# Scoring the first three heads one step earlier in an attention and soft mixture-of-experts kernel

## The chip, the cores and the metric

The kernel runs on one core of a Trainium2 chip. The metric is the time of one execution on the device in microseconds (us); less is better. The engines are named TensorE (PE in the rows; its weight loads PEld), VectorE (DVE), ScalarE (ACT) and GpSimd (POOL); SyncE (SP) issues most of the transfers.

## What is computed

Three stages follow each other, all in float32. The change lies in the first, causal attention with a decay, for 4 batches of 8 heads (32 heads, 576 positions, width 64):

```python
scores = scale * np.matmul(q, k.transpose(0, 1, 3, 2))
cum = np.cumsum(np.log(np.clip(f, 0.0001, 1.0)), axis=-1)
decay = cum[:, :, :, None] - cum[:, :, None, :]
scores = np.where(causal, -1000000000.0, scores + decay)
scores = scores - np.max(scores, axis=-1, keepdims=True)
attn = np.exp(scores)
attn = attn / (np.sum(attn, axis=-1, keepdims=True) + 1e-09)
out = np.matmul(attn, v)
```

The 2304 rows of the result (512 wide) go through a dense layer with a gate (`h * sigmoid(h)`, 2048 wide inside) and then through a soft mixture of 8 experts with 4 slots each. These two stages are not touched.

## The kernel before

**Heads come in pairs.** A pair p holds heads 2p and 2p + 1. Each pair has tiles that hold the operands of the score products over 128 partitions: `QA` and `KA` (partitions 0 to 63 the rounded queries and keys; above them rows for the decay and constant rows; partition 127 of `QA` is the **row of maxima**, which subtracts each row's maximum inside the product), and `QB` and `KB`, which hold what the rounding left over. There are three buffers of each, taken in turn (`p % 3`).

- `split_hi(p, j)` (L189) fills the rounded parts on ScalarE: j = 0 is `QA`, 1 is `KA`, 2 is `KB`; j = 3 copies `QA`'s queries into `QB` with a DMA of 288 KB. For pair 0, j = 0 makes four copies of half the size and the two copies of the decay rows (`decays_out`).
- `split_lo(p, which, h)` (L205) makes one head's remainder on GpSimd, for `QB` (which = 0) or `KB` (which = 1).
- `init_q(i)` (L133) fills buffer i of `QA`: the pad with zeros on VectorE, and partitions 64 to 127 with a DMA from buffer i - 1. That copy takes the row of maxima of buffer i - 1 along, although it is always written again before it is used.
- `spread(p)` (L213) fetches the decay rows of `KA`; from pair 2 on it reads them from `cumd`, a copy of the sums in device memory (L1127).
- `load(p)` (L169) and `load_v(p)` (L179) fetch queries and keys (576 KB) and values (320 KB).

**The work on a head.** `max_piece(i, j)` (L224), six pieces, multiplies block by block, and VectorE takes each row's maximum from the product's bank. `max_fin` (L247) transposes the maxima of a finished head (from pair 2 on of a pair) on TensorE, has VectorE copy them out as the tile `mr` and sends them by DMA (L255, 512 B a row) into partition 127 of `QA`. `s_piece(i, j)` (L265), five pieces, makes the scores, two products each, and ScalarE takes their exponential (L285). It reads all of `QA`'s partitions and so needs the row of maxima. `cut` (L295) puts zeros above the diagonal on GpSimd. `row_sums(p)` (L314) and `av(p, j)` (L336), seven pieces, make the sums and the products with the values of a pair; ScalarE copies the first of these out after j = 1 (L346), the rest after j = 6 (L348), and the sums at L323.

**The steps.** The loop of L1116 runs from step -6 to 33 and calls `att_step(i)` (L383), which walks through the words of `ORDER` (L19), the left half in even steps, the right half in odd ones. Each engine and each queue runs its instructions in the order in which they are written. `m` is a piece of the maxima of head i + 3, `s` one of the scores of head i, `v` and `r` are the values and the row sums of the pair before, `q` and `z` the roundings and remainders of a later pair, `k` cuts, `f` calls `max_fin` and sends off the row sums, `w`, `l` and `p` are the loads of values, of queries and keys, and of decays, `c` works on a weight of the next stage, and `g` calls `pump`, which issues the loads of raw weights (512 KB each, L509). So step 0 scores head 0, step 1 head 1, step 2 head 2; the values of pair 0 come in step 2. `max_fin` is also called ahead of piece 2 of the maxima in steps -2 to 1. At the start of step 0 the first load of raw weights is issued.

In steps -3 to 0 each piece of the maxima is followed by an **idle product** (`heat`, L93), which multiplies constants into a bank that nobody reads.

**The banks.** The scores take turns in three banks (`RING_A`), and the maxima, the transposes and the row sums in three others (`RING_B`); a product can start when the reader of three turns before is done.

Of the kernel before, what the change touches and what calls it, by code (L numbers as in the profile page):

```python
# [16 lines left out]
AX = mybir.AxisListType  # L17

ORDER = "m0 m1 s0 b s1 s2 m2 m3 k m4 q2 x z00 s3 m5 c q0 e s4 k v0 v1 r q1 f l g v2 v3 v4 z01 v5 v6 | m0 m1 c k k w s0 m2 s1 m3 m4 s2 z10 m5 s3 s4 n q3 p z11"  # L19
CONV_AT = (2, 6, 8, 12, 16, 18, 22, 26)  # L20
LAST = 10
SPARE = 2
# [20 lines left out]
def tile_attention_moe_softmoe(ctx: ExitStack, tc: tile.TileContext, qk, vr, f, wcat, phi, w1, w2, out):  # L43
# [89 lines left out]
    def init_q(i):  # L133
        if i == 0:
            nc.gpsimd.memset(QA[0].bitcast(F32), 0.0)
            nc.gpsimd.memset(QA[0][64:66].bitcast(F32), 1.0)
        else:
            nc.vector.memset(QA[i][0:64, :, 0:64].bitcast(F32), 0.0)
            nc.sync.dma_start(out=QA[i][64:128].bitcast(F32), in_=QA[i - 1][64:128].bitcast(F32))

    KD = []

# [239 lines left out]

    def att_step(i, cv):  # L383
        p, h = divmod(i, 2)
        s = 0 <= i < NH
        pa = p - 1
        a = 0 <= pa < NPAIR
        mi = i + 3
        mx = 0 <= mi < NH

        def cvt(n, ph):
            if ph == 0:
                conv_b(n)
            elif ph == 1:
                conv_c(n)
            elif ph == 2:
                conv_d(n, 0)
                conv_d(n, 1)
            elif ph == 3:
                conv_wh(n)  # L400
            elif ph == 4:
                conv_d(n, 2)
                conv_d(n, 3)
            elif ph == 6:
                conv_wl(n)
                conv_f(n)

        for op in ORDER.split("|")[h].split():
            k, j = op[0], op[1:]
            if k == "s" and s:  # L410
                s_piece(i, int(j))
                if i == 0 and j == "2":
                    split_hi(2, 2)
            elif k == "m" and mx:
                if j == "2" and -2 <= i <= 1:
                    max_fin()
                max_piece(mi, int(j))
                if i < 1:
                    heat(1, 256, "b0" if i < 0 else "ava")
            elif k == "v" and a:  # L420
                av(pa, int(j))
            elif k == "r" and a and done["r"] <= pa:
                row_sums(done["r"])
                done["r"] += 1
            elif k == "q" and p != 0 and 0 <= p + 2 < NPAIR:
                split_hi(p + 2, (1, 2, 0, 3)[int(j)] if p < 0 else int(j))
            elif k == "z" and (j[0] == "1" and i < 0 or i == 0):
                pass
            elif k == "z" and 0 <= (i + 3) // 2 < NPAIR:
                split_lo((i + 3) // 2, int(j[0]), int(j[1]))  # L430
            elif k == "f":
                max_fin()
                while GATHER:
                    GATHER.pop()()
            elif k == "n" and done["n"] < min(done["r"], NPAIR - 1):
                norm_b(done["n"])
                done["n"] += 1
            elif k == "b" and done["b"] < done["x"] and done["b"] in READY:
                norm_c(done["b"])
                done["b"] += 1  # L440
            elif k == "p" and 1 < p + 3 < NPAIR:
                spread(p + 3)
            elif k == "x" and done["x"] < done["n"]:
                norm_x(done["x"])
                done["x"] += 1
            elif k == "c":
                for n, ph in cv:
                    cvt(n, ph)
            elif k == "e" and -4 < i < 0:
                heat(4, 256)  # L450
            elif k == "k":
                cut()
            elif k == "g":
                pump()
            elif k == "w" and 0 <= p + 1 < NPAIR:
                load_v(p + 1)
            elif k == "l" and 3 <= p + 3 < NPAIR:
                load(p + 3)
# [651 lines left out]
    with tc.manual_schedule():  # L1110
# [5 lines left out]
        for i in range(-6, NH + 2):  # L1116
            if i == -6:
                load(0)
                load(1)
                load(2)  # L1120
                decays_in(0)
                decays_in(1)
                heat(1, 256)
                spread(0)
                init_q(1)
                spread(1)
                nc.sync.dma_start(out=cumd, in_=cum.bitcast(F32))  # L1127
                init_q(2)
            if i in (0, 3, 5):
                mo["cap"] += 1  # L1130
            if i == 0:
# [5 lines left out]
            cv = [(n, i - b) for n, b in enumerate(CONV_AT) if 0 <= i - b < 7]  # L1137
            att_step(i, cv)
            if i == -2:
                split_lo(0, 1, 0)  # L1140
                split_lo(0, 1, 1)
                split_lo(1, 1, 0)
                split_lo(1, 1, 1)
            elif i == -1:
                nc.scalar.activation(warm, nbias[0:1], AF.Exp)
                for j in (0, 1, 3):
                    split_hi(2, j)
                split_lo(1, 0, 0)
                split_lo(1, 0, 1)
            if i == NH + SEL:  # L1150
                mo.update(last=LAST)
                pump()
# [255 lines left out]
```

## Time and profile before

| what | us |
|---|---|
| median of 3 runs | 499.40 |
| lowest and highest run | 499.32, 499.78 |
| the profiled execution | 499.37 |
| its span in the profile | 497.7 |

The profile is one execution taken by the hardware's profiler. The span runs from the first instruction to the last; the profiled execution's own time is 1.67 us longer. Idle time is put down to what released the engine last. Rows of the timeline begin with the start and the duration in us, both from the span's start; rows that stand for several instructions end in their count, and their duration is that of the whole group.

### The profile page before, as it was taken

How to read it: one execution, taken by the hardware profiler on the slowest of the kernel's cores; microseconds unless marked ns; L12 is line 12 of the kernel's file. 1: busy time of each engine (PE TensorE's matmuls, PEld its weight loads, DVE VectorE, ACT ScalarE, POOL GpSimd, SP SyncE). 2: the span in 40 equal slices, each digit the busy share in tenths (PEclk: the TensorE clock that was granted, in tenths of full speed). 3: DMA queues.
4: the chain of work that ended last, by engine and by line, in shares of the span. 5: the costliest groups of instructions: out<-in, count | busy, mean ns of one | idle time of the engine just before them, and what ended most of it. 6: DMA issues, size and time to landing. Idle time of an engine off the chain costs nothing.

```text
span 497.7 us, 11075 instructions
## 1 busy us (share of the span) xinstructions
PE 480.0 (96%) x4030; PEld 354.9 (71%) x4030; DVE 326.4 (66%) x897; ACT 259.4 (52%) x521; POOL 167.9 (34%) x219
## 2 busy tenths in 40 slices
PE   8999999999899999999999999999999999999994
PEld 4787877787787778777777677677666767755562
DVE  7767788778677549999977765666655533253133
ACT  7889889899888567454434333133312323231022
POOL 9978898889788610022300000000000000022000
PEclk9999999999999999999999999999999999999997
DMA  6837665656464349765759799998987989979997
GB/s 187 220 103 201 180 197 182 197 150 190 130 202 113 82 142 400 266 197 145 207 155 296 239 279 283 319 331 291 288 280 237 303 290 412 410 262 384 408 392 262
DMA packets 57111, 122.12 MB, mean 245 GB/s; under 512 B 9794, under 2 KB 28514, under 8 KB 57056
## 3 DMA queue, kind: packets, MB, share of 16 engines
q1 hardware_dynamic: 55712, 117.21, 71.7%
q0 software_dynamic: 1344, 4.20, 3.0%
q8 instruction: 32, 0.52, 0.4%
q14 instruction: 23, 0.19, 0.1%
HBM read 90.45 MB, written 25.39 MB: 233 GB/s over the span
## 4 chain that ended last, share of the span: by engine, by line
PE 83%; DVE 5%; DMA 4%; ACT 3%; issue 2%; POOL 1%; SPq 1%; DVEq 0%; ACTq 0%; POOLq 0%
PE h L654 12%; PE h L656 12%; PE h L655 12%; PE av L341 9%; PE mx L233 5%; PE rs L320 5%; PE st L279 4%; PE st L281 4%; PE lp L761 3%; PE pp L898 3%; PE so L1036 3%; PE h L974 3%; DMA gr<-far 2%; DVE junk L239 2%; DMA WO<-wb 1%
## 5 line engine op out<-in xcount | busy, mean ns | idle before, releaser
L654 PE MATMUL h<-w,xh 128*128 128x512 f32 x280 | 114.7, 410 | 0.0
L656 PE MATMUL h<-w,xh 128*128 128x512 f32 x280 | 110.5, 395 | 0.0
L655 PE MATMUL h<-w,xl 128*128 128x512 f32 x280 | 110.3, 394 | 0.0
L285 ACT ACTIVATE E<-st 128x256 f32<-128x256 f32 (+4 forms) x160 | 63.1, 430 | 10.6 <-PE st L281 6.1
L239 DVE CUSTOM_DVE_ANT_0 junk<-mx,mask 128x64 bf16<-128x64 f32 (+3 forms) x128 | 49.9, 414 | 27.3 <-PE mx L233 25.8
L654 PEld LDWEIGHTS h<-w,xh 128*128 128x128 f32 x280 | 52.6, 188 | 16.5 <-issue 4.9
L656 PEld LDWEIGHTS h<-w,xh 128*128 128x128 f32 x280 | 52.7, 188 | 12.5
L655 PEld LDWEIGHTS h<-w,xl 128*128 128x128 f32 x280 | 52.7, 188 | 11.0
L821 POOL COPY arena<-arena 128x128 f32<-128x128 f32 x4 | 1.1, 294 | 172.9 <-ACT gt L671 157.9
L279 PE MATMUL st<-QA,KA 128*128 128x256 f32 (+2 forms) x192 | 56.3, 303 | 2.3 <-ACT E L285 0.8
L671 ACT ACTIVATE gt<-h 128x512 f32<-128x512 f32 x38 | 22.7, 597 | 64.4 <-PE h L656 61.7
L680 DVE SCALAR_TENSOR_TENSOR gt<-gt,h 128x512 f32<-128x512 f32 x38 | 26.0, 684 | 44.7 <-ACT gt L671 44.7
L233 PE MATMUL mx<-KA,QA 127*128 127x64 f32 (+2 forms) x192 | 50.6, 329 | 2.2 <-ACT KA L203 1.3
L281 PE MATMUL st<-QB,KB 128*128 128x256 f32 (+2 forms) x192 | 51.6, 293 | 0.0
L341 PE MATMUL av<-E,VF 128*64 128x320 f32 (+4 forms) x448 | 50.8, 364 | 0.0
L302 POOL TENSOR_SCALAR_AFFINE_SELECT E<-E 128x256 f32<-128x256 f32 (+1 forms) x96 | 41.6, 449 | 21.4 <-ACT E L285 19.6
L211 POOL TENSOR_TENSOR QB<-qk,QA 64x576 fp32r<-64x576 f32 x30 | 42.7, 1425 | 2.3
L209 POOL TENSOR_TENSOR KB<-qk,KB 64x576 fp32r<-64x576 f32 x30 | 42.3, 1430 | 1.0
L341 PEld LDWEIGHTS av<-E,VF 128*64 128x64 f32 x448 | 29.5, 136 | 17.8 <-POOL E L302 0.3
L668 ACT ACTIVATE gt<-h 128x512 f32<-128x512 f32 x32 | 19.1, 596 | 40.5 <-PE h L656 40.4
L279 PEld LDWEIGHTS st<-QA,KA 128*128 128x128 f32 x192 | 34.6, 180 | 7.2 <-ACT E L285 6.2
L733 DVE STREAM_TRANSPOSE gb<-gt 128x1024 f32<-128x1024 f32 x31 | 37.5, 1228 | 2.5 <-DMA WO<-wb 2.5
(179 smaller groups left out, 782.8 us busy)
## 6 DMA issues: line engine op xcount, KB each, us to landing
unit<-in_w_dram SPq DMA_DIRECT2D x64, 512.0 KB
raw<-in_w_dram SPq DMA_DIRECT2D x32, 512.0 KB
far<-gb SPq DMA_DIRECT2D x108, 128.0 KB
gr<-far SPq DMA_DIRECT2D x27, 512.0 KB
qk<-in_qk_dram SPq DMA_DIRECT2D x14, 576.0 KB
VF<-in_v_dram SPq DMA_DIRECT2D x16, 320.0 KB
QB<-QA SPq DMA_DIRECT2D x16, 288.0 KB
RB<-R SPq DMA_DIRECT2D x32, 144.0 KB
```

Of the source, the lines that this page charges most:

```text
L209: eng.tensor_tensor(KB.of(p)[0:64, h], src[64:128], KB.of(p)[64:128, h], ALU.subtract)
L211: eng.tensor_tensor(QB.of(p)[64:128, h], src[0:64], QA[p % 3][0:64, h, 64:640], ALU.subtract)
L233: nc.tensor.matmul(t[:, 0:w], lhsT=qa[0:127, h, 128 * blk:128 * blk + 128], rhs=ka[0:127, h, k0:k0 + w], start=True, stop=True)
L239: nc.vector.tensor_tensor_reduce(out=junk[:, 0:w], in0=t[:, 0:w], in1=mask[:, 448 - w:448], scale=1.0, scalar=Mx[p][:, h] if j == 5 else - ...
L279: nc.tensor.matmul(t[0:m, o:o + n], lhsT=ka[:, h, k0:k0 + m], rhs=qa[:, h, 64 + q0:64 + q1], start=True, stop=False)
L281: nc.tensor.matmul(t[0:m, o:o + n], lhsT=kb_[:, h, k0:k0 + m], rhs=qb[:, h, q0:q1], start=False, stop=True)
L285: nc.scalar.activation(e[0:m], t[0:m, 0:o], AF.Exp, scale=0.125)
L302: nc.gpsimd.affine_select(out=e, in_=e, pattern=pattern, compare_op=ALU.is_ge, fill=0.0, base=0, channel_multiplier=-1)
L341: nc.tensor.matmul(AVP[p][x][64 * h:64 * h + 64, o0:o0 + n], lhsT=VF[p % 2][:, kb, h], rhs=E[2 * p + h][kb][:, c:c + n], start=kb == 0, st ...
L654: nc.tensor.matmul(o, lhsT=xh[:, d, tok], rhs=w[:, 0], start=(d == 0), stop=False)
L655: nc.tensor.matmul(o, lhsT=xl[:, d, tok], rhs=w[:, 0], start=False, stop=False)
L656: nc.tensor.matmul(o, lhsT=xh[:, d, tok], rhs=w[:, 1], start=False, stop=(d == 3))
```

## The change

The words of steps -1 to 2 are replaced by a list of their own, `OPENING`. In steps -1, 0 and 1 the head that is scored is i + 1, so heads 0, 1 and 2 are each scored one step earlier and step 2 scores none. The maxima and the scores are written alternately, the maxima first. The first two pieces of pair 0's values (`V`) go to the end of step 1, around head 2's last scores. Idle products stay in steps -3 to -1 only, and in step -1 they write into another bank. The calls of `max_fin` at `f` in steps -2 and 0 go, so that the rows of heads 1 and 3 are made ahead of piece 2 in the steps that follow.

The preparation moves too. Pair 0's `split_hi` 0 and 3 go to step -6, the copy into `QB` ahead of the first `init_q`. `init_q` copies partitions 64 to 126, without the row of maxima. `init_q(2)` goes from step -6 to the end of step -1, the write of `cumd` to the end of step -2, where also the exponential's table is loaded now. Of pair 2, `split_hi` 0 goes to the end of step -2, 1 to the end of step -1, 3 to the end of step 0, and 2 into step 2 (`y`); its remainders of `KB` go from step 1 to the end of step 2.

```diff
--- before.py
+++ after.py
@@ -17,6 +17,10 @@
 AX = mybir.AxisListType
 
 ORDER = "m0 m1 s0 b s1 s2 m2 m3 k m4 q2 x z00 s3 m5 c q0 e s4 k v0 v1 r q1 f l g v2 v3 v4 z01 v5 v6 | m0 m1 c k k w s0 m2 s1 m3 m4 s2 z10 m5 s3 s4 n q3 p z11"
+OPENING = {-1: "m0 m1 k m2 w m3 s0 m4 s1 m5 s2 s3 s4 q3 p",
+           0: "m0 m1 s0 m2 s1 m3 k s2 m4 s3 m5 s4 k l g f",
+           1: "m0 m1 k w s0 m2 s1 m3 s2 m4 V0 s3 m5 s4 V1 p",
+           2: "m0 m1 b k x z00 q0 k r m2 q1 m3 l g v2 m4 v3 z01 y q2 m5 v4 v5 f v6 c"}
 CONV_AT = (2, 6, 8, 12, 16, 18, 22, 26)
 LAST = 10
 SPARE = 2
@@ -136,7 +140,7 @@
             nc.gpsimd.memset(QA[0][64:66].bitcast(F32), 1.0)
         else:
             nc.vector.memset(QA[i][0:64, :, 0:64].bitcast(F32), 0.0)
-            nc.sync.dma_start(out=QA[i][64:128].bitcast(F32), in_=QA[i - 1][64:128].bitcast(F32))
+            nc.sync.dma_start(out=QA[i][64:127].bitcast(F32), in_=QA[i - 1][64:127].bitcast(F32))
 
     KD = []
 
@@ -382,7 +386,8 @@
 
     def att_step(i, cv):
         p, h = divmod(i, 2)
-        s = 0 <= i < NH
+        si = i + (-1 <= i <= 1)
+        s = 0 <= si < NH and i != 2
         pa = p - 1
         a = 0 <= pa < NPAIR
         mi = i + 3
@@ -405,31 +410,34 @@
                 conv_wl(n)
                 conv_f(n)
 
-        for op in ORDER.split("|")[h].split():
+        for op in OPENING.get(i, ORDER.split("|")[h]).split():
             k, j = op[0], op[1:]
             if k == "s" and s:
-                s_piece(i, int(j))
-                if i == 0 and j == "2":
-                    split_hi(2, 2)
+                s_piece(si, int(j))
             elif k == "m" and mx:
                 if j == "2" and -2 <= i <= 1:
                     max_fin()
                 max_piece(mi, int(j))
-                if i < 1:
-                    heat(1, 256, "b0" if i < 0 else "ava")
+                if i < 0:
+                    heat(1, 256, "b0" if i < -1 else "ava")
+            elif k == "V":
+                av(0, int(j))
             elif k == "v" and a:
                 av(pa, int(j))
             elif k == "r" and a and done["r"] <= pa:
                 row_sums(done["r"])
                 done["r"] += 1
-            elif k == "q" and p != 0 and 0 <= p + 2 < NPAIR:
+            elif k == "q" and p != 0 and 0 <= p + 2 < NPAIR and (p > -2 or j == "1"):
                 split_hi(p + 2, (1, 2, 0, 3)[int(j)] if p < 0 else int(j))
-            elif k == "z" and (j[0] == "1" and i < 0 or i == 0):
+            elif k == "z" and (j[0] == "1" and i < 0 or 0 <= i < 2):
                 pass
             elif k == "z" and 0 <= (i + 3) // 2 < NPAIR:
                 split_lo((i + 3) // 2, int(j[0]), int(j[1]))
+            elif k == "y":
+                split_hi(2, 2)
             elif k == "f":
-                max_fin()
+                if i > 0:
+                    max_fin()
                 while GATHER:
                     GATHER.pop()()
             elif k == "n" and done["n"] < min(done["r"], NPAIR - 1):
@@ -1120,12 +1128,12 @@
                 load(2)
                 decays_in(0)
                 decays_in(1)
+                split_hi(0, 0)
                 heat(1, 256)
                 spread(0)
+                split_hi(0, 3)
                 init_q(1)
                 spread(1)
-                nc.sync.dma_start(out=cumd, in_=cum.bitcast(F32))
-                init_q(2)
             if i in (0, 3, 5):
                 mo["cap"] += 1
             if i == 0:
@@ -1137,16 +1145,22 @@
             cv = [(n, i - b) for n, b in enumerate(CONV_AT) if 0 <= i - b < 7]
             att_step(i, cv)
             if i == -2:
-                split_lo(0, 1, 0)
-                split_lo(0, 1, 1)
-                split_lo(1, 1, 0)
-                split_lo(1, 1, 1)
+                nc.sync.dma_start(out=cumd, in_=cum.bitcast(F32))
+                nc.scalar.activation(warm, nbias[0:1], AF.Exp)
+                for p in range(2):
+                    split_lo(p, 1, 0)
+                    split_lo(p, 1, 1)
+                split_hi(2, 0)
             elif i == -1:
-                nc.scalar.activation(warm, nbias[0:1], AF.Exp)
-                for j in (0, 1, 3):
-                    split_hi(2, j)
+                init_q(2)
+                split_hi(2, 1)
                 split_lo(1, 0, 0)
                 split_lo(1, 0, 1)
+            elif i == 0:
+                split_hi(2, 3)
+            elif i == 2:
+                split_lo(2, 1, 0)
+                split_lo(2, 1, 1)
             if i == NH + SEL:
                 mo.update(last=LAST)
                 pump()
```

## Rows read from the trace of the kernel before

**Rows 1.** The page, part 4: the chain that ended last, by engine.
```profile
PE 83%; DVE 5%; DMA 4%; ACT 3%; issue 2%; POOL 1%; SPq 1%; DVEq 0%; ACTq 0%; POOLq 0%
```

**Rows 2.** Busy time by stretch; the last columns are granted clock, DMA share, GB/s.
```profile
core 0: us, PE busy (x) PEld busy (x) DVE busy (x) ACT busy (x) POOL busy (x), PEclk, DMA share, GB/s
...
14.00:20.00 6.00, 5.49 (x36) 4.25 (x35) 5.19 (x24) 5.39 (x9) 5.94 (x5) 1.00 0.83 208
20.00:26.00 6.00, 5.93 (x41) 5.51 (x43) 4.62 (x23) 4.10 (x10) 5.55 (x11) 1.00 0.80 240
```

**Rows 3.** The chain of waits, 13 to 36 us: start, duration, what.
```profile
20.34 0.27 PE mx L233 x2
...
22.89 0.28 PE mx L233 x2
23.17 0.32 PE st L279
...
25.68 0.80 PE av L341 x8
26.48 1.54 PE rs L320 x34
28.02 0.21 PE mtp L252
28.23 2.21 PE av L341 x20
...
33.02 0.60 ACT E L285
...
35.87 0.36 PE av L341
```

**Rows 4.** ScalarE's timeline, 14 to 34 us.
```profile
14.06 1.15 ACT L203 ACTIVATE QA<-qk 64x1152 fp32r<-64x1152 f32 x1
...
18.20 1.16 ACT L203 ACTIVATE KB<-qk 64x1152 fp32r<-64x1152 f32 x1
...
28.64 0.39 ACT L323 ACTIVATE RS<-rs 128x288 f32<-128x288 f32 x1
...
30.48 0.44 ACT L348 ACTIVATE UB<-av 128x320 f32<-128x320 f32 x1 [0.26 <-PE av L341]
...
31.57 2.41 ACT L285 ACTIVATE E<-st 128x256 f32<-128x256 f32 x6
```

**Rows 5.** SP's queue, 12 to 20 us: start and duration of the issue.
```profile
12.81 2.13 SPq L255 DMA_DIRECT2D QA<-mr  x2
14.99 0.42 SPq L182 DMA_DIRECT2D VF<-in_v_dram  x1
...
16.75 0.64 SPq L193 DMA_DIRECT2D QB<-QA  x1
17.45 0.58 SPq L509 DMA_DIRECT2D raw<-in_w_dram  x1
18.13 1.23 SPq L255 DMA_DIRECT2D QA<-mr  x1
```

**Rows 6.** Transfers in 12.5-14.25, 15-15.75, 18.25-20, 20-21.75, 21.75-22.5 us.
```profile
DMA packets 64, 0.33 MB, mean 187 GB/s; under 512 B 0, under 2 KB 0, under 8 KB 64
...
DMA packets 69, 0.08 MB, mean 108 GB/s; under 512 B 26, under 2 KB 36, under 8 KB 69
...
DMA packets 170, 0.36 MB, mean 203 GB/s; under 512 B 22, under 2 KB 22, under 8 KB 169
...
DMA packets 134, 0.48 MB, mean 275 GB/s; under 512 B 12, under 2 KB 12, under 8 KB 134
...
DMA packets 45, 0.07 MB, mean 89 GB/s; under 512 B 23, under 2 KB 33, under 8 KB 44
```

**Rows 7.** GpSimd's timeline, remainders and cuts.
```profile
17.23 2.78 POOL L211 TENSOR_TENSOR QB<-qk,QA 64x576 fp32r<-64x576 f32 x2
...
33.22 1.06 POOL L302 TENSOR_SCALAR_AFFINE_SELECT E<-E 128x256 f32<-128x256 f32 x3
```

**Rows 8.** VectorE's timeline, the row of head 2.
```profile
17.74 0.28 DVE L254 CAST mr<-mtp 5x128 fp32r<-5x128 f32 x1 [0.51 <-PE mtp L252]
```

## The prediction

> **What bounds the kernel now.** I read the page first. TensorE carries 83% of the chain that ended last [rows 1], so the kernel is a queue of matmuls and a change of the opening can only move the point from which that queue runs without holes. The busy time by stretches shows where that point lies: TensorE is busy 5.49 us of 14 to 20, idle products included, and 5.93 of 20 to 26; the granted clock is 1.00 (2.4 GHz) in both, so nothing here is to be won from the clock. ScalarE is busy 5.39 and 4.10 us of the two times 6.00 [rows 2]: not far behind TensorE.
>
> Then the chain of waits, from 20 to 36 us [rows 3]: the maxima of head 4 start step 1 at 20.34, those of head 5 start step 2 at 22.89, head 2's scores start at 23.17, the first values at 25.68, the row sums at 26.48, the other values at 28.23 (2.21 us, to 30.43). After that the chain goes through ScalarE: at 33.02 TensorE waits for an exponential. The reader is to see why in ScalarE's timeline [rows 4]: the last copy of the values' sums ends at 30.92 (30.48 + 0.44), and from there the weight conversion and the exponentials of head 3 run back to back. **So the state of the kernel as it leaves the opening is the time at which that copy ends, 30.92 us.** Later pairs repeat this pattern, so I take it that a shift of this copy shifts everything behind it and the end.
>
> Last, SP's queue and the transfers [rows 5, 6]. SP issues head 2's row of maxima at 18.13, behind 512 KB of raw weights (17.45) and the 288 KB of QB for pair 2 (16.75). In 18.25 to 20 and 20 to 21.75 no packet lies between 512 B and 2 KB (22 and 22, 12 and 12: completions); in 21.75 to 22.5 there are ten (33 less 23): the two rows of maxima, five packets of 512 B each. The 2.5 KB issued at 18.13 land at about 22.3. The same is seen earlier: rows issued at 12.81 appear in 15 to 15.75 (36 less 26), behind the QB copy. Transfers pass in the order of issue. Before, this cost nothing: head 2's scores start at 23.17.
>
> **The change, part by part.** *Same place on its engine.* The four copies and the decays of pair 0 stay first on ScalarE; the exponential's table is loaded after the same copy as before; the pads of QA(2) move to VectorE's place after head 2's maxima, where it next waits for TensorE (as for the 0.51 us ahead of 17.74 [rows 8]). Nothing for all three. The six idle products of step 0 go: their cover is that scores fill TensorE there; if it is gone (the hold below), TensorE pauses for some 2 us, longer than any pause here, with the clock to lose; that stays in the range's upper end.
>
> *Head 0 and 1 sooner.* QB(0) is copied before head 0's maxima instead of behind those of two heads, so head 0's scores wait only for its own row, and I estimate them ready by the time ScalarE is free for them. ScalarE then sets the pace: QA(2) 14.06 to 15.2, five exponentials 2.05 (six took 2.41), the copy of KA(2) 1.16, five more 2.05 [rows 4]: 20.5. TensorE would reach head 2's scores at about 20.2, 3 us sooner than now. The transposes of heads 1 and 3 go from their steps' ends into the next steps, where the numbers to be turned are ready; TensorE waits less, inside the same 3 us.
>
> *Rows copied without the maxima.* 63 rows instead of 64: the copies no longer touch what the maxima write, so nothing waits for that. But the copy into QA(2) moves from the start of the program to the end of step -1, on SP between the load of pair 2's decays and the raw weights, where QB(2) was. SP's queue there becomes: values, QB(1), decays, QA(2), raw, head 2's row, the load of pair 3, QB(2). The load of pair 3 (and with it ScalarE's first copy in step 2) comes sooner, which removes a short wait.
>
> *The hold.* Head 2 is scored in step 1 now, so its row of maxima is wanted at 20.2. Its issue stays at about 18.1 (VectorE copies it out at 17.74 now [rows 8], and is through with head 2's maxima hardly sooner in the new order) and stays behind the raw weights. Ahead of it lie the same transfers as before, but QA(2) in place of QB(2): a copy of this kind took 12.5 to 14.25 (0.33 MB at 187 GB/s [rows 6]), about 0.25 us more than the QB it replaces. The values' load is issued some 0.2 us later than at 14.99 [rows 5], as the row of head 1 ahead of it is. So the row lands at R = 22.3 + 0.2 + 0.25 = 22.75, and TensorE, in order, stands at head 2's first score from about 20.2 on. Bounds of R: 20.2, if nothing holds it, and 24.1 (third rival). I take 22.75, since its nearest row is the same transfer behind the same load.
>
> *What follows R.* TensorE in step 1: the piece of the step before from 20.34 to 22.89, less two maxima (0.27), 2.28; the transpose 0.21; the first values 0.80: R + 3.29. Step 2: two maxima 0.28, row sums 1.54: R + 5.1. ScalarE can copy the row sums only then: 0.39; behind it stand three copies of 1.16 (KA(3), KB(2), KB(3); KB(2) was done at 18.20 and now comes here), then the copy of the values 0.44: R + 5.1 + 0.39 + 3.48 + 0.44 = R + 9.41. TensorE itself would be through at R + 5.1 + 0.56 (four maxima at 0.14) + 0.21 + 2.21 = R + 8.1 and is not last. With R = 22.75 the copy ends at 32.16 instead of 30.92: **+1.24 us**.
>
> *GpSimd* gets KB(2) only at R + 7.8 = 30.6 (two copies after the sums), does four subtractions (2 x 2.78, in pairs as at 17.23) and head 3's cuts (1.06 as at 33.22) [rows 7]: 30.6 + 5.56 + 1.06 = 37.2; the values of pair 1 are due at 35.87 + 1.24 = 37.1 and need only the first of these cuts, at about 36.6. It hides, with half a us to spare; gone, it costs what it is late.
>
> **The sum.** The profiled execution took 499.37 us (span 497.7 and 1.67 around it), the median of the runs is 499.40. 499.37 + 1.24 = 500.6. A shift of 0.2%, 1.0 us, is about what a measurement of this kernel can tell from none.
>
> **The rivals.** *Head 2's row is not held (faster).* The one mechanism: the row's packets, on few engines, pass the raw weights. Then R is 20.2 and the copy ends at 20.2 + 9.41 = 29.6: -1.3 us, 498.1. It decides from R under 20.5 (a gain over 1.0). Against it: both rows of [rows 6] waited for what was ahead. For it: all else of the change works this way, and my order of issue may be wrong in one place. 0.22.
>
> *The queue drains sooner (no change).* The transfers ahead overlap better than in a row: the 20 to 21.75 stretch ran at 275 GB/s, 18.25 to 20 at 203 [rows 6]; at the former rate throughout, the 1.47 MB (320, 288, 315 and 512 KB) from 16.2 on end at 21.5, R = 21.8, and the copy at 31.2: +0.3 us; with pieces of both, 499.2 to 500.0. 0.18.
>
> *The 63 rows spread worse (slower still).* 64 packets went evenly over sixteen engines, four each, in 1.75 us [rows 6]; if 63 go over nine, seven each, the copy takes 3.06, R = 24.06 and the copy of the values ends at 33.47: 501.9. For it: no row shows a large copy whose count sixteen does not divide, so nothing excludes it; against it, copies within one half of the partitions seem held by something other than the number of engines (187 GB/s at a share of 98.7%, where loads reach over 270), and the other seven engines get on with the raw weights meanwhile. 0.12. The Trainium skill, "DMA: Bandwidth & Descriptors", section "Why a DMA increments its semaphore by 16 and not by 1", gives this rule: the largest number up to 16 that divides the outer sizes, hence nine for 63 and sixteen for 64. By that rule this rival's time would stand; no run here shows a count that 16 does not divide at this size.
>
> That the change does not do what it says is in the forecast: heads 0 and 1 are scored sooner, head 2 only by 0.4 us.
>
> **How the numbers follow.** Forecast, the row held to 22.1 to 23.4: 0.48, own range 500.0 to 501.3, of which about two thirds lie over 500.4. Slower: 0.31 + 0.12 = 0.43, and 0.01 for the clock: 0.44. Faster: 0.22 and 0.01 for a drain below 21: 0.23. Same: the rest, 0.33. The range runs from 498.5 (leaving out most of the first rival's 0.22) to 501.8 (leaving out half of the third's), so 8 in 10.
>
> **What would show it.** Right: head 0's scores on TensorE at 14 to 15 us; a wait of TensorE of 1.5 to 2.5 us in 20 to 23 us, ended by a transfer, with ScalarE idle beside it; 512 B packets of head 2's row at 22 to 23; ScalarE's last copy of pair 0's values at about 32. Wrong: no such wait and that copy at 29 to 30 us (first rival); packets of the 63 rows spread over 3 us (third). The forecast falls if the copy moves by over 1 us and the end does not follow it.

## The result and the profile after

| | before | after |
|---|---|---|
| median of 6 runs each, us | 499.4 | 505.43 |
| lowest and highest run | 498.36, 499.78 | 503.65, 507.96 |
| the profiled execution | 499.37 | 505.82 |
| its span | 497.7 | 503.6 |

The changed kernel is slower: ratio 1.0125, 95% interval 1.0094 to 1.0156. That is +6.0 us where the forecast had +1.24 and the range ended at +2.4.

The page of the changed kernel, part 2 (40 slices of 12.6 us: busy tenths of TensorE, granted clock) and part 4, which answers to [rows 1]:

```profile
PE   8599999999999999999999999999999999999995
...
PEclk9979999999999999999999999999999999999998
...
PE 83%; DVE 4%; DMA 4%; ACT 2%; issue 2%; SPq 1%; POOL 1%; DVEq 0%; ACTq 0%; POOLq 0%
```

The shares by engine hardly differ from before, and reading stops there too early. The slices show where to look: the second one (12.6 to 25 us) has TensorE half idle, the third (25 to 38 us) has it busy at a lower clock. All that is new lies in the opening.

TensorE's timeline of the changed kernel, 13.5 to 26 us (the bracket is the idle time ahead and what ended it):

```profile
14.88 0.36 PE L283 MATMUL st<-QA,KA 128*128 128x256 f32 x1
...
24.01 0.44 PE L237 MATMUL mx<-KA,QA 127*128 127x64 f32 x2 [3.67 <-DMA QA<-QA]
25.24 0.55 PE L283 MATMUL st<-QA,KA 128*128 128x256 f32 x1 [0.80 <-DMA QA<-mr]
```

Head 0 is scored from 14.88 on. Then TensorE stands for 3.67 us at the first maxima of step 1 (head 4's), until the copy into QA(2) lands, and for 0.80 us at head 2's first score, until its row of maxima lands. That first score, R in the forecast, comes at 25.24 instead of 22.75.

SyncE's queue (answers to [rows 5]):

```profile
17.31 0.95 SPq L143 DMA_DIRECT2D QA<-QA  x1
18.31 0.47 SPq L517 DMA_DIRECT2D raw<-in_w_dram  x1
18.89 0.78 SPq L259 DMA_DIRECT2D QA<-mr  x1
```

The copy is issued at 17.31 and is there for TensorE at 24.01, 6.7 us later. The row is issued at 18.89, behind the raw weights. The trace also has the counts of each transfer's semaphore, the counter that the waiting engine reads: they come in as shares, one for each transfer engine that took part. Of the copy's nine shares eight were in by 22.79 us and the ninth at 23.88; of the row's five, four by 24.13 and the fifth at 25.11. TensorE starts 0.13 us after the last share both times. So 1.1 us of the first wait and the whole of the second hung on one late share.

Busy time by stretch (columns as in [rows 2]: the last three are granted clock, share of the transfer engines, GB/s):

```profile
14.00:16.00 2.00, 2.00 (x16) 1.57 (x15) 2.00 (x10) 1.64 (x4) 2.00 (x3) 1.00 0.04 9
...
20.00:22.00 2.00, 0.34 (x4) 0.23 (x3) 0.53 (x2) 0.72 (x3) 1.90 (x7) 1.00 1.03 214
22.00:24.00 2.00, 0.00 (x0) 0.02 (x1) 0.00 (x0) 0.00 (x0) 0.00 (x0) 1.00 0.85 232
24.00:25.00 1.00, 0.44 (x2) 0.28 (x2) 0.53 (x4) 0.00 (x0) 0.00 (x0) 0.80 1.03 396
25.00:26.00 1.00, 0.76 (x4) 0.70 (x4) 0.00 (x0) 0.00 (x0) 0.00 (x0) 0.50 1.11 204
...
31.00:32.00 1.00, 1.00 (x8) 0.62 (x7) 0.58 (x3) 0.66 (x3) 0.59 (x2) 0.79 0.06 23
32.00:34.00 2.00, 2.00 (x47) 1.64 (x46) 0.48 (x5) 1.63 (x3) 1.92 (x2) 1.00 0.00 0
```

In 22 to 24 us no engine works; everything waits for transfers. After that pause, within 24 to 25 us, the granted clock falls from 1.00 (2.4 GHz) to 0.50 (1.2 GHz), and it is back within 31 to 32. And in 14 to 16 us, before the copy is issued, the transfer engines are idle (share 0.04).

The chain of waits (answers to [rows 3]):

```profile
25.24 0.55 PE st L283
...
28.45 1.05 PE av L345 x4
...
32.07 1.54 PE rs L324 x34
33.61 0.55 PE mx L237 x2
34.16 0.69 PE av L345 x4
34.84 0.33 PE mx L237
35.17 0.69 PE av L345 x4
35.86 0.33 PE mx L237
36.19 1.01 PE av L345 x8
37.21 0.20 PE mtp L256
37.41 0.27 PE av L345 x4
...
43.12 0.80 PE av L345 x8
```

Two things are to be seen beside the wait. At half clock the first four value products take 1.05 us (28.45); the same four take 0.58 at full clock (in e4 below). And at full clock, from 33.61 on, the maxima that stand before and between the values take 0.55 (two of them), 0.33 and 0.33 us, where the forecast counted 0.14 apiece.

ScalarE's timeline (answers to [rows 4]):

```profile
26.11 0.38 ACT L289 ACTIVATE E<-st 128x256 f32<-128x256 f32 x1 [5.28 <-PE st L285]
...
37.72 0.44 ACT L352 ACTIVATE UB<-av 128x320 f32<-128x320 f32 x1 [0.19 <-PE av L345]
```

The last copy of pair 0's values ends at 38.16 (37.72 + 0.44); before, it ended at 30.92 [rows 4]. The first values of pair 1 come at 43.12 instead of 35.87 [rows 3]: **the opening is 7.25 us longer**, and the span 5.9 us.

### The profile page after: what moved, and what is told of

Read it like the earlier page. It is cut to its first block, busy times and chain, and to the rows that moved or that the text cites. A ratio compares the mean times of both kernels' runs of the same rounds, so it can differ in the third digit from the quotient of the medians.

```text
span 503.6 us, 11057 instructions
## 1 busy us (share of the span) xinstructions
PE 483.7 (96%) x4024; PEld 355.8 (71%) x4024; DVE 326.9 (65%) x897; ACT 259.1 (51%) x521; POOL 167.0 (33%) x219
## 4 chain that ended last, share of the span: by engine, by line
PE 83%; DVE 4%; DMA 4%; ACT 2%; issue 2%; SPq 1%; POOL 1%; DVEq 0%; ACTq 0%; POOLq 0%
PE h L662 12%; PE h L664 12%; PE h L663 12%; PE av L345 9%; PE mx L237 5%; PE rs L324 5%; PE st L283 4%; PE st L285 4%; PE pp L906 3%; PE lp L769 3%; PE h L982 3%; PE so L1044 2%; DVE junk L243 2%; ACT E L289 1%; DMA WO<-wb 1%
## 5 line engine op out<-in xcount | busy, mean ns | idle before, releaser
L664 PEld LDWEIGHTS h<-w,xh 128*128 128x128 f32 x280 | 52.7, 188 | 12.5
L283 PE MATMUL st<-QA,KA 128*128 128x256 f32 (+2 forms) x192 | 57.4, 308 | 3.0 <-DMA QA<-mr 0.8
L237 PE MATMUL mx<-KA,QA 127*128 127x64 f32 (+2 forms) x192 | 52.0, 333 | 5.8 <-DMA QA<-QA 3.7
L679 ACT ACTIVATE gt<-h 128x512 f32<-128x512 f32 x38 | 22.7, 596 | 64.1 <-PE h L664 58.7
L345 PE MATMUL av<-E,VF 128*64 128x320 f32 (+4 forms) x448 | 52.3, 368 | 0.0
L306 POOL TENSOR_SCALAR_AFFINE_SELECT E<-E 128x256 f32<-128x256 f32 (+1 forms) x96 | 40.5, 440 | 28.1 <-ACT E L289 26.7
L237 PEld LDWEIGHTS mx<-KA,QA 127*128 127x128 f32 x192 | 33.4, 192 | 11.3 <-issue 4.2
```

The lines of the kernel that those rows point to most:

```text
L237: nc.tensor.matmul(t[:, 0:w], lhsT=qa[0:127, h, 128 * blk:128 * blk + 128], rhs=ka[0:127, h, k0:k0 + w], start=True, stop=True)
L283: nc.tensor.matmul(t[0:m, o:o + n], lhsT=ka[:, h, k0:k0 + m], rhs=qa[:, h, 64 + q0:64 + q1], start=True, stop=False)
L306: nc.gpsimd.affine_select(out=e, in_=e, pattern=pattern, compare_op=ALU.is_ge, fill=0.0, base=0, channel_multiplier=-1)
L345: nc.tensor.matmul(AVP[p][x][64 * h:64 * h + 64, o0:o0 + n], lhsT=VF[p % 2][:, kb, h], rhs=E[2 * p + h][kb][:, c:c + n], start=kb == 0, st ...
L664: nc.tensor.matmul(o, lhsT=xh[:, d, tok], rhs=w[:, 1], start=False, stop=(d == 3))
```

## The experiments

All numbers of one kind are in this table; first values is the start of pair 1's values in the chain of waits, R the start of head 2's first score. Each ratio is to the kernel before in the same series (its medians there: 498.97 for e1 to e4, 498.48 for e5 to e8, 498.71 for e9, 498.98 for e12); it is worked out from all the single times and so can differ a little from the ratio of the medians. The last three columns are read from one profiled execution of each kernel. How far such a reading can stray is seen in e4, which has the same transfers as the changed kernel: its maxima of head 4 start at 23.37 us, those of the changed kernel at 24.01.

| run | median us | ratio, 95% interval | R | end of last copy | first values |
|---|---|---|---|---|---|
| before | 499.40 | | 23.17 | 30.92 | 35.87 |
| after | 505.43 | 1.0125 [1.0094, 1.0156] | 25.24 | 38.16 | 43.12 |
| e1_rows | 503.65 | 1.0095 [1.0071, 1.0119] | 24.19 | 36.86 | 41.81 |
| e2_raw | 502.87 | 1.0095 [1.0060, 1.0129] | 23.91 | 36.53 | 41.49 |
| e3_both | 501.11 | 1.0042 [1.0027, 1.0057] | 22.53 | 34.21 | 39.18 |
| e4_heat | 503.55 | 1.0093 [1.0072, 1.0114] | 24.96 | 35.12 | 40.09 |
| e7_early | 501.52 | 1.0050 [1.0033, 1.0068] | 23.03 | 33.19 | 38.14 |
| e8_early_rows | 501.56 | 1.0063 [1.0042, 1.0084] | 22.72 | 34.42 | 39.37 |
| e6_early_all | 498.58 | 1.0007 [0.9990, 1.0024] | 21.24 | 31.40 | 36.36 |
| e5_before63 | 500.48 | 1.0037 [1.0017, 1.0057] | | 32.46 | 37.69 |
| e9_best | 497.62 | 0.9990 [0.9973, 1.0007] | 20.57 | 31.02 | 36.00 |
| e12_grouped | 498.31 | 0.9989 [0.9971, 1.0008] | 20.71 | 30.89 | 36.12 |

**e1_rows: the copy of 63 rows as 48 and 15.** The changed kernel with:

```diff
-            nc.sync.dma_start(out=QA[i][64:127].bitcast(F32), in_=QA[i - 1][64:127].bitcast(F32))
+            for part in (slice(64, 112), slice(112, 127)):
+                nc.sync.dma_start(out=QA[i][part].bitcast(F32), in_=QA[i - 1][part].bitcast(F32))
```

> The changed kernel with the copy of 63 rows split into one of 48 and one of 15 rows. Theory A (63 rows spread over few transfer engines, which holds QA(2) and, in the order of issue, head 2's row behind it): TensorE's wait for QA(2) shrinks from 3.7 us to about 1, head 2's row lands at about 22.8 us instead of 25.2, the clock falls little or not at all, 500.3 to 501.5 us. Theory B (the number of rows is indifferent, the raw weights ahead of head 2's row are the hold): both waits stay as they are, 505 us.

The wait for the copy falls from 3.67 to 2.48 us, it lands at 23.00 instead of 24.01, and R moves from 25.24 to 24.19. So the form with 63 rows costs 1.05 us of R here, and it is not the whole: R stays 1.44 us over the forecast. By theory A the wait was to shrink to about 1 us.

**e2_raw: the raw weights behind head 2's row.** The first `pump` goes, so that the load is issued by the `g` at the end of step 0.

```diff
-            if i == 0:
-                pump()
```

> The changed kernel with the first load of raw weights issued at the end of step 0, behind head 2's row and the load of pair 3. Theory A: QA(2) still lands at about 24 us, so TensorE waits as long for it; only the second wait of 0.8 us goes; 504 to 505 us. Theory B: head 2's row lands at 20 to 21 us, 498 to 499 us.

The wait for the row is gone, that for the copy falls to 3.04 us, and R is 23.91: 1.33 us sooner. The copy, issued ahead of the 512 KB, also lands 0.6 us sooner (23.40) when they do not follow it. That this is due to them is not shown: in e4, where they do follow it, it landed as early (23.37).

**e3_both: both edits.** (e1's lines and e2's together.)

```diff
+            for part in (slice(64, 112), slice(112, 127)):
...
-            if i == 0:
-                pump()
```

> Both edits: 48 and 15 rows, and the raw weights behind head 2's row. Theory A and the hold of the prediction together: QA(2) at about 21 us, head 2's row at 21 to 21.5 us, clock at 1.00 throughout, 498.5 to 499.7 us. If the loss lies elsewhere in the new order (the copies of ScalarE in step 2, GpSimd's cuts), it stays over 501.

R is 22.53, 2.71 us sooner; the two alone gave 1.05 and 1.33, 2.38 together. Beside e2, the rows are worth 1.38 us here. The wait for the copy is 1.71 us, and the clock still fell. Busy time by stretch of this run:

```profile
21.00:22.00 1.00, 0.00 (x0) 0.00 (x0) 0.02 (x2) 0.04 (x1) 0.97 (x4) 1.00 0.87 199
...
23.00:24.00 1.00, 1.00 (x5) 1.00 (x5) 0.87 (x5) 0.37 (x1) 0.00 (x0) 0.50 1.02 287
```

TensorE does nothing in 21 to 22, and runs at 1.2 GHz from 22.9 to 26.3 us.

**e4_heat: idle products in the pause.** The changed kernel with 28 idle products at the end of step 0, which keep TensorE at work while the transfers are out.

```diff
             elif i == 0:
                 split_hi(2, 3)
+                heat(28, 256, "ava")
```

> The changed kernel with 28 idle products of 256 columns between steps 0 and 1, in the stretch in which TensorE waits for QA(2) (20.3 to 24.0 us). If the half clock after the wait is a loss of its own: the waits stay (head 4's first maxima at 24.0, head 2's first score at 25.2), the clock stays at 1.00, the row sums start at about 28.8 instead of 32.1, 502 to 503 us, and the runs scatter less. If the clock costs nothing that ScalarE doesn't cost anyway: 505 us.

Busy time by stretch of this run:

```profile
22.00:24.00 2.00, 1.81 (x15) 1.31 (x13) 0.32 (x3) 0.00 (x0) 0.00 (x0) 1.00 0.86 252
24.00:26.00 2.00, 1.04 (x7) 1.04 (x8) 0.62 (x4) 0.39 (x1) 0.00 (x0) 1.00 1.05 287
26.00:28.00 2.00, 2.00 (x13) 1.35 (x13) 1.25 (x5) 0.98 (x2) 0.41 (x1) 1.00 0.84 164
```

And its TensorE timeline:

```profile
23.37 0.44 PE L237 MATMUL mx<-KA,QA 127*128 127x64 f32 x2
24.96 0.36 PE L283 MATMUL st<-QA,KA 128*128 128x256 f32 x1 [1.15 <-DMA QA<-mr]
```

The clock stays at 1.00. R is 24.96, only 0.28 us sooner than in the changed kernel, but the first values of pair 1 come 3.03 us sooner (40.09). The difference, 2.75 us, is what the half clock cost the opening. From R to those values it is 15.13 us here and 17.88 in the changed kernel (43.12 - 25.24). The first four value products, 1.05 us in the changed kernel, in its chain of waits:

```profile
26.75 0.58 PE av L345 x4
```

The times show less of it: 4.6 us over the kernel before in place of 6.0, with intervals that overlap.

**e7_early: the copy of 63 rows one step sooner.** Into the stretch in which the transfer engines were idle.

```diff
                 split_hi(2, 0)
-            elif i == -1:
                 init_q(2)
+            elif i == -1:
```

> The changed kernel with one thing moved: the copy into QA(2) (still 63 rows) is issued at the end of step -2, where the transfer engines idle at 14 to 16 us, instead of the end of step -1. Theory now: the time of this copy in a queue full of loads is the main cause, and head 2's row then waits only for the values, QB(1) and the raw weights. Expected: no wait for QA(2), head 2's row at 21 to 22 us, a wait of TensorE of 1 to 2 us at half or full clock, the first values of pair 1 at 36 to 38 us (35.87 before, 43.12 changed), 499.5 to 501.5 us. Rival (the raw weights are the main cause): the row lands after 23 us and the time stays over 503.

The copy is issued at 13.29 instead of 17.31. TensorE's timeline:

```profile
21.77 0.44 PE L237 MATMUL mx<-KA,QA 127*128 127x64 f32 x2 [1.44 <-DVE Mt L243]
23.03 0.36 PE L283 MATMUL st<-QA,KA 128*128 128x256 f32 x1 [0.82 <-DMA QA<-mr]
```

R is 2.21 us sooner; there are two pauses of 1.44 and 0.82 us in place of 3.67 and 0.80, and the clock stays at 1.00. The first values come 4.98 us sooner: 2.21 of R and 2.77 of the clock. The trace puts the first pause down to VectorE. It was not the copy either: its last share was in at 17.31 us. What came in just before those maxima, at 21.68, is the last share of KA(2)'s decay rows, which they read too; these were issued at 16.82.

**e8_early_rows: e7 and e1 together.**

```diff
+            for part in (slice(64, 112), slice(112, 127)):
...
                 init_q(2)
+            elif i == -1:
```

> As the last, with the copy split into 48 and 15 rows. If the count of rows matters where the queue has room: the row of head 1 behind it and the values land sooner by up to 1 us and the time is 0 to 1 us under that of the last. If it matters only under load: the same time.

The first pause is gone: those maxima start at 20.27, and KA(2)'s decay rows had landed at 20.16 instead of 21.68. Whether that is due to the split of the copy ahead of them is not shown: in both runs the copy itself had landed by 17.34. But R gained only 0.31 us (22.72): the row of maxima is now waited for in one piece, 2.00 us, and the clock fell to 0.50 in 23 to 26 us, so the first values come 1.23 us later than in e7. In these two executions, then, two short pauses cost less than a single one that is not as long as their sum; the medians of the two kernels are the same (501.52 and 501.56).

**e6_early_all: e1, e2 and e7 together.**

```diff
+            for part in (slice(64, 112), slice(112, 127)):
...
-            if i == 0:
-                pump()
...
                 init_q(2)
+            elif i == -1:
```

> All three: the copy into QA(2) at the end of step -2, in 48 and 15 rows, and the raw weights behind head 2's row. The first rival of the prediction, with nothing held: head 2's row at 19.5 to 20.5 us, no wait of TensorE over 0.8 us, clock 1.00, ScalarE's last copy of pair 0's values at 29.6 to 30.3 us (30.92 before), first values of pair 1 at 34.5 to 35.3, 498 to 498.8 us: faster than both kernels by a little. If something else in the new order costs: over 499.5 us.

TensorE's timeline:

```profile
21.24 0.36 PE L284 MATMUL st<-QA,KA 128*128 128x256 f32 x1 [0.15 <-DMA QA<-mr]
```

ScalarE's timeline:

```profile
26.94 0.41 ACT L328 ACTIVATE RS<-rs 128x288 f32<-128x288 f32 x1 [0.34 <-PE rs L325]
...
30.96 0.44 ACT L353 ACTIVATE UB<-av 128x320 f32<-128x320 f32 x1 [0.19 <-PE av L346]
```

The pause is 0.15 us and the clock is 1.00. This is the case of the first rival, the row that is not held: R is 21.24 (it said 20.2) and the copy ends at 31.40 (it said 29.6). The time is that of the kernel before. So with the holds taken away the change gains nothing, which no step of the forecast had said.

**e5_before63, e11_48, e10_31: the copies alone, in the kernel before.** The same line with 63 rows, with 48 and 15, and with 32 and 31; of the last two there is one execution each.

```diff
-            nc.sync.dma_start(out=QA[i][64:128].bitcast(F32), in_=QA[i - 1][64:128].bitcast(F32))
+            nc.sync.dma_start(out=QA[i][64:127].bitcast(F32), in_=QA[i - 1][64:127].bitcast(F32))
...
+            for part in (slice(64, 112), slice(112, 127)):
...
+            for part in (slice(64, 96), slice(96, 127)):
```

> The kernel before with nothing changed but the copies of 63 rows instead of 64. SP's queue waits for the first of these copies to land before it issues the second, so the second's issue time measures the first's landing: 11.38 us with 64 rows, issued at 7.96. Theory A (63 rows go over fewer engines): the second is issued at 12.3 to 12.8 us, and all that stands behind it on SP moves by as much; the end 0 to 1 us later. Theory B (the count is indifferent): 11.4 us and 499 us.

> The kernel before with the copy made as two, of 48 and 15 rows. If the count sets the engines (16 and 15), the second pair is issued at 11.4 to 11.7 us, at most the extra issue (0.5 to 0.7 us) later than 11.38 and before the 12.07 of 63 rows. If splitting itself costs a landing of its own: at 12 us or later.

> The kernel before with the copy of 64 rows made as two, of 32 and 31 rows. SP waits for the first pair to land before it issues the second pair (11.38 us with 64 rows in one, 12.07 with 63). If a copy goes over as many engines as divide its count (31: one), the 31 rows of 5 KB pass one after the other: one engine moved at most some 28 GB/s where all were full, so 155 KB take over 5.5 us and the second pair is issued at 15 us or later. If the count is indifferent: at 11.5 to 12.2 us.

The second copy reads what the first has written, so its issue in SyncE's queue tells when the first had landed (where a copy is made in two parts, each part waits for the part with the same rows); the first is issued at 7.96 or 7.97 in all four. In the kernel before, with 64 rows:

```profile
11.38 0.54 SPq L139 DMA_DIRECT2D QA<-QA  x1
```

with 63 rows (e5):

```profile
12.07 0.81 SPq L139 DMA_DIRECT2D QA<-QA  x1
```

with 48 and 15 (e11):

```profile
11.54 1.53 SPq L140 DMA_DIRECT2D QA<-QA  x2
```

with 32 and 31 (e10; both parts in one row, the second part only after some 18 us):

```profile
12.14 6.55 SPq L140 DMA_DIRECT2D QA<-QA  x2
```

Busy time by stretch of that run:

```profile
10.50:11.50 1.00, 0.72 (x5) 0.55 (x4) 1.00 (x8) 0.97 (x2) 1.00 (x1) 1.00 0.06 20
```

63 rows land 0.7 us later than 64, less than theory A said. Of the 48 and 15 the 48 land 0.16 later, but the 15, issued behind them at 8.61, only at 11.80, by their semaphore: 0.5 us later than the 64 rows (11.31 there) and 0.2 sooner than the 63 (12.00). And 31 rows need several us: 31 x 5120 B is 159 KB, which at 20 GB/s takes 7.9 us, and a share of 0.06 is one engine of 16. The semaphore of the 31 rows was full at 18.04. The shares tell the number of engines: 16 came in for 64, 48 and 32 rows, 15 for 15, nine for 63 and one for 31 (where there are fewer than 16, one more count stands some 0.4 us behind the issue). In e5 head 0's score waited 1.00 us for its row of maxima, which stands behind the second copy in the queue, the last copy of pair 0's values ended 1.5 us later, and the time rose by 0.37%. e10 took 512.02 us, e11 498.74 (before, in that series, 498.71), although its last copy of pair 0's values ended 0.8 us later than before, at 31.71.

**e9_best: the holds away and ScalarE lighter.** e6, with the copy of KB(2) moved from step 2 to the end of step 0, where ScalarE is idle, and the load of pair 0's values (`W`) issued behind head 2's row of maxima.

```diff
-OPENING = {-1: "m0 m1 k m2 w m3 s0 m4 s1 m5 s2 s3 s4 q3 p",
-           0: "m0 m1 s0 m2 s1 m3 k s2 m4 s3 m5 s4 k l g f",
+OPENING = {-1: "m0 m1 k m2 m3 s0 m4 s1 m5 s2 s3 s4 q3 p",
+           0: "m0 m1 s0 m2 s1 m3 k s2 m4 s3 m5 s4 k W l g f",
...
-           2: "m0 m1 b k x z00 q0 k r m2 q1 m3 l g v2 m4 v3 z01 y q2 m5 v4 v5 f v6 c"}
+           2: "m0 m1 b k x z00 q0 k r m2 q1 m3 l g v2 m4 v3 z01 q2 m5 v4 v5 f v6 c"}
...
             elif i == 0:
+                split_hi(2, 2)
                 split_hi(2, 3)
```

> The kernel with all three edits (copy into QA(2) at the end of step -2 in 48 and 15 rows, raw weights behind head 2's row), and two more: the copy of KB(2) on ScalarE at the end of step 0, where it idles, instead of in step 2, and the values of pair 0 loaded behind head 2's row. If the time from head 2's first score to the last copy of pair 0's values (10.16 us in all runs at full clock) is ScalarE's queue, it falls by about 1.1 us; head 2's row lands at 20.3 to 20.8 us; that copy ends at 29.5 to 30 us (30.92 before), the first values of pair 1 at 34.4 to 34.9 us, 497.5 to 498 us. If ScalarE is not what is last there, it ends where it did (31.4 less what the row gains), 498.5 us.

R is 20.57, 2.6 us sooner than before, with no pause at all, and the last copy ends at 31.02, 0.1 us later than before. It waits for TensorE's values although ScalarE has one copy of 1.16 us less in that step:

```profile
30.58 0.44 ACT L353 ACTIVATE UB<-av 128x320 f32<-128x320 f32 x1 [0.63 <-PE av L346]
```

From R to the end of the copy are 10.45 us (10.16 in e6). ScalarE does not set this end, TensorE does.

**e12_grouped: maxima and values in groups.** e9 with one order changed:

```diff
-           2: "m0 m1 b k x z00 q0 k r m2 q1 m3 l g v2 m4 v3 z01 q2 m5 v4 v5 f v6 c"}
+           2: "m0 m1 b k x z00 q0 k r m2 q1 m3 l g v2 v3 z01 q2 m4 m5 v4 v5 f v6 c"}
```

> The kernel of the run before (e9_best) with one order changed: in the second step of the opening the maxima of pair 1 and the values of pair 0 stand in groups and no longer take turns. In the changed kernel a group of maxima between two groups of value products took 0.33 to 0.55 us of TensorE in the chain, where my forecast counted 0.14. Theory: the turns cost this. Then grouping shortens the stretch from head 2's first score to the last copy of pair 0's values: the copy ends at about 30.3 to 30.6 us (31.02 before it), the first values of pair 1 come at 35.3 to 35.6 (36.00), and the time is 497.0 to 497.6 us. Rival: the maxima cost the same wherever they stand, or TensorE waits for VectorE or for a bank instead; then the copy ends at 31.0 again and the time is about 497.6.

TensorE's timeline of e9, from the first of these maxima to the next step:

```profile
26.34 0.62 PE L238 MATMUL mx<-KA,QA 127*128 127x320 f32 x2
26.89 0.76 PE L346 MATMUL av<-E,VF 128*64 128x320 f32 x4
27.63 0.40 PE L238 MATMUL mx<-KA,QA 127*128 127x288 f32 x1
...
30.46 0.47 PE L238 MATMUL mx<-KA,QA 127*128 127x64 f32 x2
```

The same of e12:

```profile
26.46 0.62 PE L238 MATMUL mx<-KA,QA 127*128 127x320 f32 x2
27.01 1.30 PE L346 MATMUL av<-E,VF 128*64 128x320 f32 x8
28.24 0.53 PE L238 MATMUL mx<-KA,QA 127*128 127x288 f32 x2
...
30.33 0.47 PE L238 MATMUL mx<-KA,QA 127*128 127x64 f32 x2
```

The same products take 3.87 us instead of 4.12, so two turns fewer are worth 0.25 us, and the copy ends 0.27 us sooner counted from R (10.18). That it is the turns fits, but less was gained than expected: the copy ends at 30.89, not at 30.3 to 30.6, and the first values of pair 1 are no sooner (36.12). The time is not told apart from that of e9 or of the kernel before.

## Why the prediction was wrong

Right were the sign, the mechanism in part (head 2's scores held by transfers in SyncE's queue, ScalarE idle beside them), head 0's scores at 14.9, and that the table load, the pads and GpSimd cost nothing that shows. The size was wrong by 6.0 us in the opening. The terms add up:

| step of the forecast | said | measured | us over the forecast |
|---|---|---|---|
| R | 22.75 | 25.24 | 2.49 |
| from R to the end of the copy, at full clock | 9.41 | 10.16 (e4, e6, e7) | 0.75 |
| half clock, to pair 1's first values | hardly any | 17.88 less 15.12 (e6) | 2.76 |
| sum, beside the 1.24 forecast | | | 6.00 |

1.24 + 6.00 = 7.24, and 7.25 was measured.

**R: "a copy of this kind took 12.5 to 14.25 ... about 0.25 us more than the QB it replaces".** This step failed in three ways. First, the count of rows: the third rival, that the 63 rows spread worse, was true, and it should have been a term of the sum and not a rival to it. It was given 0.12 with the argument that something other than the number of engines holds such copies. That argument is not refuted: one engine alone moved 20 GB/s (e10), sixteen together 187 [rows 6], 12 each, so nine could move nearly as much as sixteen. This would fit that the count cost 0.7 us in the idle queue (e5) and not the 1.31 of the rival. It costs 1.05 us of R by e1, 1.38 by e3 beside e2. The Trainium skill, "DMA: Bandwidth & Descriptors", section "Why a DMA increments its semaphore by 16 and not by 1", has the rule (the largest number up to 16 that divides the outer sizes: sixteen for 64 and 48, nine for 63, one for 31), and these runs agree with it: the shares above, and in order 11.38, 11.54 (the 48 rows alone), 12.07 and some 18 us. Second, the forecast saw the copy only as something ahead of the row in the queue. But head 4's maxima, the first work of step 1, read QA(2) too, so TensorE stood at 20.34 for the copy itself. From the issue to the landing were 6.7 us, 5.5 with 48 and 15 (17.50 to 23.00), where such a copy took 3.4 in the idle queue of the kernel before (7.96 to 11.38). Third, the base of the sum: 22.3 is where the packets of head 2's row lie in the kernel before, but its semaphore was full only at 23.00, just ahead of head 2's scores (23.17). So the row came with no time to spare already, and the sum started 0.7 us too early. What of the rest of R is due to the load ahead of the copy and to the late share of one engine was not tried.

**From R to the copy: "TensorE itself would be through at R + 8.1 ... and is not last".** It is last: the copy waits for values in every run of the new order. Maxima and values take turns in step 2, 4.07 us from 33.61 to 37.68 in the chain where the forecast had 2.98 (0.56 + 0.21 + 2.21), and what lies before, from R to the end of the row sums, took 5.61 us in e6 (21.24 to 26.85) and not 5.1. Of the 0.75 us only 0.19 are TensorE's being last, by the wait of e6's copy; the other 0.56 would have come by ScalarE's queue too, which starts with the late row sums (26.94, R + 5.70, for R + 5.1). A sign of the turns stood in the chain of the kernel before and was not read: right behind values two maxima took 0.39 us at 30.43, behind scores 0.28 at 22.89 [rows 3].

```profile
30.43 0.39 PE mx L233 x2
```

e12 shows the cause for part of it, 0.25 us for two turns. The Trainium skill, "TensorEngine Tiling (Array Packing)", section "Tiling Modes", says that a change of the tiling mode drains the engine. The times agree with such a cost: maxima fill 128 columns of the array, while the value products of the two heads, 64 columns each (127\*128 and 128\*64 in the rows), run side by side, 7 ns apart in the trace. In e9 the weight load of the maxima begins at 27.62, together with its product, just as those values end; behind scores it begins ahead of it. The width alone does not do it: the maxima at 22.89 stand behind scores of 64 columns, one product at a time, and no such cost is seen there. That a change of mode is the reason was not tested by itself.

**The clock: "with the clock to lose; that stays in the range's upper end".** It was seen and given 0.01 and no price. The pause came to 3.67 and 0.80 us, the clock was at 1.2 GHz for some seven us behind it, and that alone cost 2.76 us in the opening, more than twice the whole forecast. The six idle products that the change takes out stood in step 0, ahead of the pause; e4 put 28 into the pause itself and had the 2.75 us of the opening back.

**"A shift of this copy shifts everything behind it and the end."** This held for the most part. From the end of the copy to the first values of pair 1 there are 4.95 us before and 4.96 after. The opening's 7.25 us are 5.9 in the span and 6.0 between the medians; about one us is regained in later stages, and where was not traced further. Opening and time agree only so far: e4, e5 and e7 lie 0.2 to 0.8 us further over the kernel before in their medians than in their openings, e1 to e3 and after 1.2 to 1.7 us less far.

**What the forecast did not ask.** Whether an earlier R could bring anything. It took R + 9.41 as a gain for an R of 20.2, and e9 has R at 20.57 and no gain. TensorE was busy 5.93 of 6.00 us in 20 to 26 [rows 2]: where it is full, scoring a head sooner puts other products of TensorE behind it. Before, 7.75 us lay between R and the end of the copy (23.17 to 30.92); in e9 10.45 do. That the idle products taken out were room won, and that the turns took it again, would fit, but no run separates the two.

## What to carry to other kernels

Before a copy is made smaller or moved, look at how its number of rows divides, who reads it first, and what the queue carries at its new time: one row less cost about 1 us of waiting, and a copy that was free at the start of the program cost TensorE 3.67 us when it was issued in a loaded stretch. Read a landing from the issue or the start that waited for it, not from the last packet. A pause of TensorE is priced with its clock: here the slower products behind it cost 2.8 us of the opening after pauses of 4.5 us together, and idle products in the pause gave that back. Where the bounding engine is already busy all of the time, an order that scores sooner won nothing by itself here, and maxima and values ran a little shorter in groups than in turns (0.25 us for two turns, too little for the times to show).

## What the runs showed of the hardware that was not expected

- A copy of 31 rows ran on one engine of 16 at 20 GB/s, and 63 rows landed 0.7 us later than 64 in an idle queue (e5), and about 1 us later than 48 and 15 in a loaded one (24.01 and 23.00, after and e1).
- The packets of a transfer end well before it counts as landed: by 0.3 us in an idle queue (10.97 and 11.31, the first copy of before) and by 1.1 in a loaded one (22.80 and 23.88, the copy into QA(2) of after), where one engine's share came 1.1 us behind the others.
- The clock was at 0.50 after pauses of 3.67 and 0.80 us (after), of 2.48 us (e1), of 2.00 us (e8) and of 1.71 us (e3), in e2 already within one of 3.04 us, and stayed at 1.00 after pauses of 1.44 and 0.82 us (e7); it stayed so in e4 with idle products in the pause and 1.15 us of waiting left.
- One piece of maxima between two groups of values took 0.33 us of TensorE (34.84 in after) where it takes 0.14 between scores (39.54 in the same chain).
- A wait put down to VectorE (1.44 us in e7) ended with the landing of KA(2)'s decay rows (21.68, the maxima start at 21.77): the engine that is named need not be the cause.
